# The chunk's whole decay: four small matmuls, or the last row of the running sum turned by a transfer

## Chip, cores and metric

The kernel runs on one core of one Trainium2 chip. The metric is the device time of one execution in microseconds (us). A core has TensorE (PE, with its weight loads shown as PEld), VectorE (DVE), ScalarE (ACT), GpSimd (POOL) and SyncE (SP, which here only issues transfers); each works off its own instructions in order.

## The reference, cut to what matters

```python
# q, k, v, f_logit: (4, 8, 768, 48)  float32;  w_in: (384, 2048);  w_out: (2048, 384)
f = 1.0 / (1.0 + np.exp(-f_logit))
for t in range(S):
    state = f[:, :, t, :, None] * state + np.einsum('bhd,bhe->bhde', k[:, :, t], v[:, :, t])
    y[:, :, t] = np.einsum('bhd,bhde->bhe', q[:, :, t], state)
x = y.transpose(0, 2, 1, 3).reshape(B * S, H * D)     # (3072, 384)
h = x @ w_in
out = np.maximum(0.01 * h, h) @ w_out
```

A gated linear attention (a state of 48 x 48 for each head, that decays by a gate for each of its rows) is followed by a two-layer network with a leaky ReLU.

## The kernel before

The 768 steps are cut into 6 chunks of 128. A unit `u` is one chunk `c` of one batch `b`; there are 24, ordered by chunk and then by batch, so unit 0 to 3 is the first chunk of the four batches. A unit's tile has the 128 steps on the partitions and 8 heads x 48 columns.

For each unit:

- `load` (L82 to L89) issues four transfers of 192 KB from SP: `f_raw`, `k_raw`, `q_raw`, `v_raw`.
- `gate_act`: ScalarE forms `lf = ln(1 + exp(-f))`, which is minus the logarithm of the gate. `lf` has 64 columns for each head, the last 16 zero.
- `gate_pe` (L113): one matmul with an upper triangle of ones gives the running sum of `lf` over the steps in PSUM, `cs[:, 0:384]` (L117). Four more matmuls (L120), one for each pair of heads, take `lf` of the pair as weights and a column of ones as the moving operand. Each writes one column of `cs`: the sum over the whole chunk, with the 2 x 64 features of the pair on the partitions. The last chunk needs no such sum, so 20 units of 24 do this.
- `decay_act` (L124): ScalarE reads `cs` and writes `em_t = exp(cs)`, `a_t = exp(-cs)`, and `a_end = exp(-)` of the four added columns (L133).
- `scale_pool`: GpSimd multiplies `kh = k * em_t` (L139), `qh = q * a_t` (L140) and casts `v` (L142).
- `turn_pe`, `turn_dve`, `score_pe`, `mask_dve`, `mix_pe`, `state_pe`: transposes of `kh` and `qh` (L149), scores (L168), the causal mask, and the output `y` and the chunk's addition to the state.
- `state_dve` adds it to the state `sf`; `state_pool` (L216) multiplies `sf` by `a_end`, broadcast along the free dimension (L221), and casts it (L222).
- `up` and `down`: the two layers (L250, L259), with ScalarE's leaky ReLU from PSUM (L252); `put` copies the result and stores it from SP (L265).

The order on every engine is written out by hand, with no reordering. In the prologue SP issues `load(0)` to `load(4)`; then come `gate`, `decay` and `scale` of units 0 and 1, and the rest of unit 0 with `state_pool(0)`. The loop `for i in range(24)` works on several units at once: it issues `load(i+5)`, turns unit i+1, does the first half of `up(i)`, scores i+1, does `gate_pe`, `decay_act` and `scale_pool` of unit i+2, the second half of `up(i)`, `mix_pe`, `y_act`, `state_pe`, `state_dve` and `state_pool` of i+1, `gate_act` of i+3, `down(i)` with the transposes `x_pe(i+1)` (L233) in its middle, and `put(i)`. So GpSimd has, in this order: `scale_pool(0)`, `scale_pool(1)`, `state_pool(0)`, `scale_pool(2)`, `state_pool(1)`, `scale_pool(3)`, and so on.

The PSUM tiles `cs`, `py`, `pt` and `px` of a pass share a ring of two buffers (`tag="sm"`): `pt` (L203) takes the buffer that `cs` leaves.

Of the kernel before, what the change touches and what calls it, by code (L numbers as in the profile page):

```python
# [9 lines left out]
FP32 = mybir.dt.float32  # L10
BF16 = mybir.dt.bfloat16
AF = mybir.ActivationFunctionType
# [3 lines left out]
def kernel(  # L16
# [10 lines left out]
    nc = tc.nc  # L27

    B, H, S, D = q.shape
    assert (B, H, S, D) == (4, 8, 768, 48)  # L30
    C = 128
    NCH = S // C
    P2 = H // 2
# [7 lines left out]
    const = ctx.enter_context(tc.tile_pool(name="const", bufs=1))  # L41
    inp = ctx.enter_context(tc.tile_pool(name="inp", bufs=6))
    work = ctx.enter_context(tc.tile_pool(name="work", bufs=3))
# [14 lines left out]
    make_upper_triangular(nc, ut, val=1.0, diag=True)  # L58
    ident = const.tile([128, 128], BF16, tag="ident")
    make_identity(nc, ident)  # L60
    ones_col = const.tile([128, 1], BF16, tag="ones")
    nc.gpsimd.memset(ones_col, 1.0)

    w_in_b = const.tile([128, NK, FF], BF16, tag="w_in")
    w_out_b = const.tile([128, NF, KD], BF16, tag="w_out")
# [2 lines left out]
    lfs = [const.tile([128, H, 64], BF16, name=f"lf{i}", tag=f"lf{i}") for i in range(3)]  # L68
    qhs = [const.tile([128, H, 64], BF16, name=f"qh{i}", tag=f"qh{i}") for i in range(3)]
    khs = [const.tile([128, H, 64], BF16, name=f"kh{i}", tag=f"kh{i}") for i in range(3)]  # L70
    qbds = [const.tile([128, P2, 2, 128], BF16, name=f"qbd{i}", tag=f"qbd{i}") for i in range(2)]
    state_f = [const.tile([128, P2, D], FP32, name=f"sf{b}", tag=f"sf{b}") for b in range(B)]
    state_b = [const.tile([128, P2, D], BF16, name=f"sb{b}", tag=f"sb{b}") for b in range(B)]
    for t in lfs + qhs + khs + qbds:
        nc.vector.memset(t, 0.0)
    for t in state_f:
        nc.vector.memset(t, 0.0)


# [23 lines left out]
    st = {}  # L103
# [9 lines left out]
    def gate_pe(u):  # L113
        c, b = units[u]
        lf = lfs[u % 3]
        cs = ps_s.tile([128, 512], FP32, name="cs", tag="sm")
        nc.tensor.matmul(cs[:, 0:H * D], ut, lf[:, :, 0:D], start=True, stop=True)  # L117
        if c < NCH - 1:
            for p in range(P2):
                nc.tensor.matmul(cs[:, H * D + p:H * D + p + 1], lf[:, 2 * p:2 * p + 2, :], ones_col,  # L120
                                 start=True, stop=True)
        st[u] = {"cs": cs}

    def decay_act(u):  # L124
        c, b = units[u]
        cs = st[u]["cs"]
        a_t = work.tile([128, H, D], BF16, name="a_t", tag="a_t")
        em_t = work.tile([128, H, D], BF16, name="em_t", tag="em_t")
        nc.scalar.activation(em_t, cs[:, 0:H * D], AF.Exp, scale=1.0)  # L129
        nc.scalar.activation(a_t, cs[:, 0:H * D], AF.Exp, scale=-1.0)  # L130
        if c < NCH - 1:
            a_end = work.tile([128, P2], FP32, name="a_end", tag="a_end")
            nc.scalar.activation(a_end, cs[:, H * D:H * D + P2], AF.Exp, scale=-1.0)  # L133
            st[u]["a_end"] = a_end
        st[u]["a"], st[u]["em"] = a_t, em_t

    def scale_pool(u):
# [78 lines left out]
    def state_pool(u):  # L216
        c, b = units[u]
        if c == NCH - 1:
            return
        sf = state_f[b]  # L220
        nc.gpsimd.tensor_mul(sf, sf, st[u]["a_end"][:, :, None].to_broadcast([128, P2, D]))  # L221
        nc.gpsimd.tensor_copy(out=state_b[b], in_=sf)  # L222

    def y_act(u):
# [54 lines left out]
    gate_act(0)  # L279
    gate_act(1)  # L280
    gate_pe(0)
    decay_act(0)
    scale_pool(0)
    gate_pe(1)
    decay_act(1)
    scale_pool(1)
    gate_act(2)
# [6 lines left out]
    y_act(0)  # L294
    state_dve(0)
    state_pool(0)
    x_pe(0)
    x_dve(0)

    for i in range(NU):  # L300
# [11 lines left out]
        if n2 < NU:  # L312
            gate_pe(n2)
            decay_act(n2)
            scale_pool(n2)
        up(i, 2)
        up(i, 3)
        if n1 < NU:
            mix_pe(n1)
            y_act(n1)  # L320
            state_pe(n1)
            state_dve(n1)
            state_pool(n1)
# [38 lines left out]
```

## Time and profile before

| what | value |
|---|---|
| median of 3 runs | 212.48 us (212.34 to 213.68) |
| the profiled execution | 211.29 us, of which 209.4 us are the span from the first to the last instruction |
| PE busy | 177.8 us (85%) |
| PE weight loads busy | 146.1 us (70%) |
| ACT busy | 108.7 us (52%) |
| DVE busy | 97.4 us (46%) |
| POOL busy | 76.8 us (37%) |
| HBM read, written | 25.17 MB, 4.72 MB |

The profile was taken on one execution; the 1.89 us outside the span lie before the first and after the last instruction. Busy shares are means over the whole span, and the beginning differs from the rest: in the first 33 us the transfers of weights and inputs run at 176 GB/s and PE is busy for 4.77 us; from 41.5 us to 167.8 us PE is busy without a break. A matmul's end is modelled, so PE's busy time is not PE at its peak.

### The profile page before, as it was taken

To read this page: it belongs to the slowest core of one execution; us is meant where nothing else is said; L and a number is where in the kernel's file an instruction comes from. 1 tells how busy PE (TensorE), PEld (TensorE's weight loads), DVE (VectorE), ACT (ScalarE), POOL (GpSimd) and SP (SyncE) were. 2 spreads that over 40 slices of the span, in tenths; PEclk is the share of its full clock that TensorE was granted. 3 is DMA by queue.
4 is the path that set the end of the run, shared out by engine and by line. 5 is a ranking of instruction groups with operands and counts; after the bars stand their busy time and mean duration, and the time that the engine had idled before them with its cause. 6 is when DMAs were issued, how large, how long until landed. Compare 5 with 4: busy or idle time off the path is not lost.

```text
span 209.4 us, 5831 instructions
## 1 busy us (share of the span) xinstructions
PE 177.8 (85%) x2432; PEld 146.1 (70%) x2432; DVE 97.4 (46%) x223; ACT 108.7 (52%) x237; POOL 76.8 (37%) x129
## 2 busy tenths in 40 slices
PE   0000149999999999999999999999999999999993
PEld 0000028788779788877988887798888778877881
DVE  8000044466546545654654565465455545633511
ACT  4000332775576458447645845774585567555540
POOL 8300071542553255145325524532552454034000
PEclk9999999999999999999999999999999999999999
DMA  6999999998796479568647846956695681100111
GB/s 114 171 195 184 199 191 189 156 219 163 121 176 143 105 136 177 114 118 163 147 102 133 186 111 116 157 116 141 128 187 113 119 153 41 38 28 18 38 41 38
DMA packets 106267, 27.12 MB, mean 130 GB/s; under 512 B 100352, under 2 KB 105472, under 8 KB 106240
## 3 DMA queue, kind: packets, MB, share of 16 engines
q1 hardware_dynamic: 103296, 23.60, 59.5%
q0 software_dynamic: 2944, 3.15, 9.0%
q8 instruction: 19, 0.31, 0.6%
q14 instruction: 8, 0.07, 0.1%
HBM read 25.17 MB, written 4.72 MB: 143 GB/s over the span
## 4 chain that ended last, share of the span: by engine, by line
PE 83%; issue 10%; POOL 4%; DVE 1%; ACT 0%; POOLq 0%
PE pm L250 32%; PE pm L259 30%; PE pw L168 6%; PE tp L149 5%; PE py L191 2%; PE px L233 2%; PE py L187 2%; PE cs L117 2%; PE pt L203 2%; POOL w_in_b L94 2%; POOL w_out_b L99 1%; POOL kh L139 1%; PE cs L120 1%; DVE wm L175 1%; POOL qh L140 1%
## 5 line engine op out<-in xcount | busy, mean ns | idle before, releaser
L252 ACT ACTIVATE gT<-pm 128x512 bf16<-128x512 f32 x96 | 56.2, 601 | 64.1 <-PE pm L250 62.3
L250 PE MATMUL pm<-xT,w_in_b 128*128 128x128 bf16 x1152 | 73.4, 221 | 0.0
L259 PE MATMUL pm<-w_out_b,gT 128*128 128x384 bf16 x384 | 70.1, 326 | 0.0
L250 PEld LDWEIGHTS <-w_in_b 128*128 128x128 bf16 x1152 | 67.2, 99 | 0.6
L139 POOL TENSOR_TENSOR kh<-k_raw,em_t 128x384 bf16<-128x384 f32 x24 | 22.0, 916 | 110.5 <-ACT em_t L129 105.7
L259 PEld LDWEIGHTS <-gT 128*128 128x128 bf16 x384 | 35.2, 98 | 18.8
L175 DVE TENSOR_TENSOR wm<-pw,ut 128x512 bf16<-128x512 f32 x48 | 30.9, 686 | 12.7 <-PE pw L168 11.9
L117 PE MATMUL cs<-lf,ut 128*128 128x384 bf16 x24 | 8.1, 339 | 24.9 <-ACT lf L111 24.9
L264 DVE COPY osb<-pm 128x384 f32<-128x384 f32 x24 | 13.4, 558 | 26.6 <-PE pm L259 26.6
L109 ACT ACTIVATE e_t<-f_raw 128x384 f32<-128x384 f32 x24 | 12.9, 536 | 23.7 <-DMA f_raw<-in_f_logit_dram 23.7
L120 PEld LDWEIGHTS <-lf 128*128 128x128 bf16 x80 | 5.0, 99 | 25.2 <-issue 23.8
L140 POOL TENSOR_TENSOR qh<-q_raw,a_t 128x384 bf16<-128x384 f32 x24 | 21.9, 914 | 0.0
L155 DVE COPY kT<-tp 128x512 bf16<-128x512 bf16 x24 | 10.0, 415 | 23.6 <-PE tp L149 23.6
L238 DVE COPY xT<-px 128x384 bf16<-128x384 bf16 x24 | 8.6, 358 | 22.2 <-PE px L233 22.2
L213 DVE TENSOR_TENSOR sf<-sf,pt 64x192 f32<-64x192 f32 x20 | 6.9, 346 | 22.2 <-PE pt L203 22.2
L168 PE MATMUL pw<-qbd,kT 128*128 128x256 bf16 x96 | 14.8, 277 | 1.3 <-DVE qbd L158 1.3
L129 ACT ACTIVATE em_t<-cs 128x384 bf16<-128x384 f32 x24 | 11.8, 491 | 4.5 <-PE cs L120 3.7
L111 ACT ACTIVATE lf<-e_t 128x384 bf16<-128x384 f32 x24 | 12.5, 523 | 0.8
L168 PEld LDWEIGHTS <-kT 128*128 128x128 bf16 x96 | 9.4, 99 | 4.3 <-DVE kT L155 0.8
L226 ACT CAST xn<-py 128x384 bf16<-128x384 f32 x24 | 11.4, 474 | 1.5 <-PE py L191 1.5
L142 POOL CAST v_b<-v_raw 128x384 bf16<-128x384 f32 x24 | 12.1, 505 | 0.0
L130 ACT ACTIVATE a_t<-cs 128x384 bf16<-128x384 f32 x24 | 11.6, 485 | 0.0
(37 smaller groups left out, 155.3 us busy)
## 6 DMA issues: line engine op xcount, KB each, us to landing
f_raw<-in_f_logit_dram SPq DMA_DIRECT2D x24, 192.0 KB, 3.2
k_raw<-in_k_dram SPq DMA_DIRECT2D x24, 192.0 KB, 3.8
q_raw<-in_q_dram SPq DMA_DIRECT2D x24, 192.0 KB, 4.0
v_raw<-in_v_dram SPq DMA_DIRECT2D x24, 192.0 KB, 4.3
out_dram<-osb SPq DMA_DIRECT2D x24, 192.0 KB, 2.0
w_in_b<-in_moe_w_in_dram POOLq DMA_DIRECT2D x6, 256.0 KB, 8.8
w_out_b<-in_moe_w_out_dram POOLq DMA_DIRECT2D x2, 768.0 KB, 18.2
```

The costliest lines, as they stand in the source:

```text
L109: nc.scalar.activation(e, f, AF.Exp, scale=-1.0)
L111: nc.scalar.activation(lf[:, :, 0:D], e, AF.Ln, bias=1.0)
L117: nc.tensor.matmul(cs[:, 0:H * D], ut, lf[:, :, 0:D], start=True, stop=True)
L139: nc.gpsimd.tensor_mul(khs[u % 3][:, :, 0:D], r["k"], st[u]["em"])
L140: nc.gpsimd.tensor_mul(qhs[u % 3][:, :, 0:D], r["q"], st[u]["a"])
L142: nc.gpsimd.tensor_copy(out=v_b, in_=r["v"])
L168: nc.tensor.matmul(pw[:, 2 * i:2 * i + 2, :], kT[:, p, :], qbd[:, p, :, :], start=True, stop=True)
L175: nc.vector.tensor_mul(wm, pw, ut[:, None, :].to_broadcast([128, 4, 128]))
L250: nc.tensor.matmul(pm[:, i, :], w_in_b[:, kk, ff * 128:(ff + 1) * 128], s["xT"][:, kk, :], start=(kk == 0), stop=(kk == NK - 1))
L252: nc.scalar.activation(s["g"][:, 4 * g:4 * g + 4, :], pm, AF.Prelu, alpha=0.01)
L259: nc.tensor.matmul(s["pm2"], s["g"][:, ff, :], w_out_b[:, ff, :], start=(ff == 0), stop=(ff == NF - 1))
L264: nc.vector.tensor_copy(out=osb, in_=st[u]["pm2"])
```

## The change

The four matmuls on a column of ones go. The last row of the running sum already holds the sum over the chunk, but with the features along the free dimension of partition 127. ScalarE takes the exponential of the last 32 rows of `cs` (partitions 96 to 127) into a float32 tile `a_row`, written so that in each row the 128 features of a pair stand apart by four elements and the four pairs side by side. A transfer on SP's queue then moves row 127 (128 x 4 numbers, 2 KB) to a tile `a_ends` with one feature on each partition and four numbers in each. `state_pool` reads that tile. There are three `a_row` and four `a_ends` buffers, cleared by VectorE at the start.

```diff
-    ones_col = const.tile([128, 1], BF16, tag="ones")
-    nc.gpsimd.memset(ones_col, 1.0)
...
+    a_ends = [const.tile([128, P2], FP32, name=f"ae{i}", tag=f"ae{i}") for i in range(4)]
+    a_rows = [const.tile([128, 128, P2], FP32, name=f"ar{i}", tag=f"ar{i}") for i in range(3)]
-    for t in lfs + qhs + khs + qbds:
+    for t in a_ends + lfs + qhs + khs + qbds:
         nc.vector.memset(t, 0.0)
-    for t in state_f:
+    for t in state_f + [t[96:128] for t in a_rows]:
         nc.vector.memset(t, 0.0)
...
         nc.tensor.matmul(cs[:, 0:H * D], ut, lf[:, :, 0:D], start=True, stop=True)
-        if c < NCH - 1:
-            for p in range(P2):
-                nc.tensor.matmul(cs[:, H * D + p:H * D + p + 1], lf[:, 2 * p:2 * p + 2, :], ones_col,
-                                 start=True, stop=True)
...
         if c < NCH - 1:
-            a_end = work.tile([128, P2], FP32, name="a_end", tag="a_end")
-            nc.scalar.activation(a_end, cs[:, H * D:H * D + P2], AF.Exp, scale=-1.0)
-            st[u]["a_end"] = a_end
+            a_row = a_rows[u % 3]
+            nc.scalar.activation(a_row[96:128].rearrange("t (i e) p -> t p i e", i=2)[:, :, :, 0:D],
+                                 cs[96:128, 0:H * D].rearrange("t (p i d) -> t p i d", p=P2, i=2),
+                                 AF.Exp, scale=-1.0)
+            nc.sync.dma_start(out=a_ends[u % 4], in_=a_row[127:128])
...
-        nc.gpsimd.tensor_mul(sf, sf, st[u]["a_end"][:, :, None].to_broadcast([128, P2, D]))
+        nc.gpsimd.tensor_mul(sf, sf, a_ends[u % 4][:, :, None].to_broadcast([128, P2, D]))
```

## The prediction, made before the changed kernel ran

> **What bounds the kernel now.** I read the page first, for the engine that ends last.
>
> ```profile
> PE 177.8 (85%) x2432; PEld 146.1 (70%) x2432; DVE 97.4 (46%) x223; ACT 108.7 (52%) x237; POOL 76.8 (37%) x129
> PE 83%; issue 10%; POOL 4%; DVE 1%; ACT 0%; POOLq 0%
> ```
>
> The second line is the chain that ended last: 83% of it is PE. After the start-up PE never idles until the last units, so PE time removed there shortens the run, and another engine matters only where PE comes to wait for it. Next I read the timeline over two passes of the loop. Passes i = 0 to 17 compute the whole decay of unit i+2; from i = 18 the unit is of the last chunk and the L120 matmuls are absent, while all else of pass 18 is there. So the profile of before already has a pass with the matmuls gone:
>
> ```profile
> 158.40 1.50 PE L250 MATMUL pm<-xT,w_in_b 128*128 128x128 bf16 x24
> ...
> 159.88 0.60 PE L168 MATMUL pw<-qbd,kT 128*128 128x256 bf16 x4
> 160.31 0.33 PE L117 MATMUL cs<-lf,ut 128*128 128x384 bf16 x1
> 160.47 0.24 PE L120 MATMUL cs<-ones_col,lf 128*128 128x1 bf16 x4
> 160.58 1.50 PE L250 MATMUL pm<-xT,w_in_b 128*128 128x128 bf16 x24
> ...
> 165.70 1.50 PE L250 MATMUL pm<-xT,w_in_b 128*128 128x128 bf16 x24
> ...
> 167.18 0.60 PE L168 MATMUL pw<-qbd,kT 128*128 128x256 bf16 x4
> 167.61 0.33 PE L117 MATMUL cs<-lf,ut 128*128 128x384 bf16 x1
> 167.78 1.50 PE L250 MATMUL pm<-xT,w_in_b 128*128 128x128 bf16 x24
> ...
> 168.73 1.18 ACT L252 ACTIVATE gT<-pm 128x512 bf16<-128x512 f32 x2
> ...
> 169.81 0.47 ACT L226 CAST xn<-py 128x384 bf16<-128x384 f32 x1
> ...
> 170.83 0.32 PEld L233 LDWEIGHTS <-xn 128*128 128x128 bf16 x3
> ```
>
> Each line is start, duration, engine, source line. From the scores (L168) to the next `up` (L250) pass 17 takes 160.58 - 159.88 = 0.70 us, pass 18 takes 167.78 - 167.18 = 0.60. The whole pass falls from 165.70 - 158.40 = 7.30 to 7.20 (the next pass opens at 172.90). Four L120 matmuls cost PE 0.10 us, not the 4 x 0.16 of their own durations: they are pipelined.
>
> Last I read the start, because the change puts a transfer into SP's queue and makes GpSimd wait for it.
>
> ```profile
> 33.17 0.51 POOL L221 TENSOR_TENSOR sf<-sf,a_end 128x192 f32<-128x192 f32 x1 [2.86 <-DVE sf L214]
> ...
> 36.44 0.98 SPq L87 DMA_DIRECT2D v_raw<-in_v_dram  x1
> 37.47 1.00 SPq L87 DMA_DIRECT2D f_raw<-in_f_logit_dram  x1
> ...
> 37.80 0.92 POOL L139 TENSOR_TENSOR kh<-k_raw,em_t 128x384 bf16<-128x384 f32 x1 [3.71 <-ACT em_t L129]
> 38.67 0.92 POOL L140 TENSOR_TENSOR qh<-q_raw,a_t 128x384 bf16<-128x384 f32 x1
> ```
>
> ```profile
> v_raw<-in_v_dram SPq DMA_DIRECT2D x1, 192.0 KB, 5.5
> f_raw<-in_f_logit_dram SPq DMA_DIRECT2D x1, 192.0 KB, 5.5
> ```
>
> The first fence shows SP still issuing the prologue's loads at 36.44 us: that `v_raw` is the last transfer of load(4), and the `f_raw` at 37.47 opens load(5). The second, the transfers issued in that stretch, gives 5.5 us from issue to landing for both. The first state multiply (L221, unit 0) ran at 33.17, before SP reached the place where the change puts unit 0's transfer.
>
> **The change part by part.**
>
> *Removed: 80 L120 matmuls and their weight loads.* 18 passes x 0.10 us. The gain of pass 0 falls ahead of the stall worked out below and is swallowed by it; 17 x 0.10 = 1.7 us remain. The eight in the prologue (units 0, 1) lie under waits for transfers and are worth nothing. From both sides: the weight-load row puts pass 18's gap at as little as 0.08, so 1.4 to 1.8.
>
> *Replaced on ScalarE: 20 exponentials of 128x4 by 20 of 32x384.* The old one's row is 0.18 us, but the next instruction starts 0.05 after it (161.51 to 161.57), so it costs the queue almost nothing. The new one has the free size of `a_t`, which starts 0.39 after `em_t` and is followed 0.37 later. No row shows an exponential that writes float32 16 bytes apart. Lower bound 0.37; upper bound 0.60, the mean duration of the 128x512 L252 with nothing overlapped. I take 0.37, since the element count is `a_t`'s. What it makes late: the two L252 and `xn` (L226). Set on pass 18: `xn` ends at 169.81 + 0.47 + 0.37 = 170.65, and PE loads it at 170.83; a hand-over takes 0.05 (ACT's `xn` of 32.05 ends at 32.53, PE starts at 32.58), so 0.13 us of cover is left and the edit costs nothing. At 0.60 the cover is gone and PE waits 0.10 per pass, 1.7 us in all. `cs` is also held longer: the new read ends about 169.2, and `pt`, which takes that buffer, starts at 169.52. Hidden.
>
> *Added on VectorE and taken from GpSimd at the start:* seven clears (three of 32x512 float32, four of 128x4) for one of 0.10 us. VectorE ends its clears near 5.2 us and first works at 28.37 (23 us of idle); by the rows of L75 and L77 (0.22 to 0.49 each) seven cost under 3.5 us, hidden there. The four that come first delay `lf`'s clear (0.86 to 1.68), which ScalarE needs at 4.28. Nothing.
>
> *Added on SP: 20 transfers of 2 KB.* Each waits for ScalarE. What is queued behind it is load(i+5) or the store `put(i)`. In the loop it stands after load(i+5) and before `put(i)`, for which SP waits anyway (89.3 us over 21 times in SP's list of waits), so the wait replaces a part of a longer one. GpSimd needs unit i+2's numbers a pass later: the exponential ends near 161.9 in pass 17, SP has issued `v_raw` by 162.3, 4.3 us (the median landing of `v_raw`) gives 166.6, and `state_pool` would read at 163.56 + 7.2 = 170.8. Four us of cover. Their 2,560 packets stand against 103,296: no bandwidth.
>
> *At the start that cover isn't there.* The program places the transfers of units 0 and 1 after load(4), so SP issues unit 0's at 37.47, though ScalarE has had the row since about 26.6. When it lands is the term that decides. The nearest rows: `v_raw` just ahead lands at 36.44 + 5.5 = 41.9, `f_raw` issued at this very place at 37.47 + 5.5 = 43.0; the store in SP's queue at 42.59 landed after 3.5 us, 46.1, 0.6 after the `v_raw` ahead of it (41.78 + 3.7 = 45.5), though later such stores, with nothing ahead, took 2.0 (median). So a transfer lands in the order of the queue. I take 42.3; bounds 39.5 (37.47 + 2.0, a free queue) and 43.0.
>
> The Trainium skill, in "DMA: Bandwidth & Descriptors", section "Queues, rings and completion order", says that each DMA engine consumes a queue's descriptors in ring order, yet that completion isn't first in, first out for the issuing engine; the same page's section on the anatomy of one DMA puts the fixed cost at about 2.0 us. By the fixed cost alone the sum would end at 211.3 us, by the landing rows at 214.1; the rows show a full queue and I follow them.
>
> GpSimd works in order, so `scale_pool(2)` stands behind `state_pool(0)`. With a landing at L: L221 starts at L + 0.05, L222 0.57 later (39.99 to 40.56 in a later pass), `kh` of unit 2 0.30 after that, `qh` 0.87 after (37.80 to 38.67), and `qh` takes 0.91. It is ready at L + 2.70 = 45.0, where before it was ready at 39.6. PE's transposes of unit 2 stood at 41.53 and 41.75, and `up(1)` at 41.98, 0.23 after the `qh` transposes. Now `up(1)` starts at L + 2.70 + 0.05 + 0.23 = L + 2.98 = 45.3. That is 3.3 us late (L - 39.0), and PE is the bound from there on. Unit 1's numbers follow unit 0's by a fraction of a us and are needed only after `scale_pool(2)`; unit 2's, behind load(5), land near 47 and are needed past 50. One stall, then.
>
> *The sum.* 211.29 + 3.3 - 1.7 = 212.9 us for an execution like the profiled one (span 209.4 to 211.0). The median of the runs stands 1.19 higher, so 212.48 + 1.6 = 214.1 us, 0.8% more than before.
>
> **A price that the trace shows only at the start: cold matmuls.** PE would idle from 41.5 to 44.2 and again until 45.1.
>
> ```profile
> 33.73 2.77 PE L250 MATMUL pm<-xT,w_in_b 128*128 128x128 bf16 x24
> ...
> 37.05 1.50 PE L250 MATMUL pm<-xT,w_in_b 128*128 128x128 bf16 x24
> ```
>
> The same 24 matmuls take 2.77 us just after the waits of the prologue and 1.50 once PE has run on; the granted clock reads 1.00 in both stretches. A stall could bring one such slow stretch back: 0 to 1.27 us. The idle time before the slow stretch was spread over 30 us, the new one is under 4 us, so I take 0 and keep 1.27 for the range. The skill's page "TensorE: Matmul & The Clock Gate", section "Why this matters for your kernels", asks for no idle gap above about 3 us, as a window of idle halves the clock; the gap of 2.7 us here is under that, and by the rule a landing half a us later would add the 1.27.
>
> **The rivals.**
>
> 1. *The stall comes and PE turns slow.* 214.1 + 1.27 = 215.4 us. For: the 2.77 us row. Against: a gap shorter than any that the trace shows ahead of slow matmuls.
> 2. *The other side: the transfer doesn't queue.* If its 2 KB land 2.0 us after issue, L = 39.5, `up(1)` is 0.5 late, and the gain of 1.7 wins: 212.48 + 0.5 - 1.7 = 211.3 us. It decides wherever L lies below 40.7, where L - 39.0 equals 1.7. For: the stores' median of 2.0, and few bytes. Against: the store at 42.59, which took 3.5 behind loads.
> 3. *The 128 runs of 16 bytes are slow.* All on one DMA engine, at the mean packet of the main queue (59.5% of 16 x 209.4 us over 103,296 packets, 19 ns), they take 2.5 us more: L = 44.8, 216.6 us. For: the source is one partition. Against: nothing in the trace shows an uneven split.
> 4. *ScalarE becomes the wait in every pass.* At 0.60 for the new exponential: 214.1 + 1.7 = 215.8 us. For: 0.13 us of cover is thin. Against: three rows of this size are followed after 0.37 to 0.39.
>
> **How the numbers follow.** Forecast 0.46, rival 1 0.20, rival 2 0.13, rival 3 0.11, rival 4 0.10. The likeliest time is 214.1; its own range, from the gain's 1.4 to 1.8 and a landing of 41.9 to 43.0, is 213.6 to 215.1. The range of all reaches down past half of the way to rival 2 and up past rival 3 with a little of the slow clock: 212.0 to 217.0. A measurement here tells about 1% from no change: below 210.4 is faster, above 214.6 slower. Faster 0.05 (rival 2 with nothing left of the 0.5). Slower 0.48: a third of the forecast's own range, nearly all of rivals 1, 3 and 4. Within 1% 0.47.
>
> **What would show each step right or wrong.** Passes of 7.20 us in place of 7.30 from the second to the 18th; L221's first start moving from 33.17 to 42 or later, its releaser a DMA; `kh` of unit 2 at 43 instead of 37.80; one wait on PE before the qh transposes, near 45; `xn` still ready before PE loads it; an ACT group of 32x384 near 0.49 us. If L221 starts before 40.7 the forecast is wrong and rival 2 holds; if the 24 matmuls after the stall take more than 2 us, rival 1; if PE shows a wait for `xn` in each pass, rival 4.

## The result: 2.6% slower, and the profile after

The changed kernel takes 218.01 us (median of 4 runs, 217.57 to 218.78) against 212.41 for the kernel before in the same comparison: a ratio of 1.0264, with a 95% interval of 1.0201 to 1.0328. That is above the range of 212.0 to 217.0. The profiled execution took 217.57 us, with a span of 215.8. Some executions of one kernel run over a per cent longer than its others in a slower state; the ratios here and below leave those out, and need not be the quotients of the medians given beside them, which include them.

Two lines of the page after the change: the busy time of each engine, and each engine's share of the chain of work that ended last:

```profile
PE 179.7 (83%) x2352; PEld 143.6 (67%) x2352; DVE 99.1 (46%) x230; ACT 125.9 (58%) x237; POOL 76.6 (36%) x128
PE 66%; ACT 14%; issue 10%; POOL 6%; DMA 2%; DVE 1%; ACTq 0%; POOLq 0%
```

ScalarE's share of the chain went from 0% to 14%; its busy time rose by 17.2 us with as many instructions as before. The groups of instructions by shape (last columns: busy us, mean ns of one, idle time before them and what ended it) show where the time went:

```profile
L131 ACT ACTIVATE ar<-cs 32x384 f32<-32x384 f32 x20 | 17.3, 863 | 0.5
L126 ACT ACTIVATE a_t<-cs 128x384 bf16<-128x384 f32 x24 | 11.6, 484 | 0.0
L221 POOL TENSOR_TENSOR sf<-sf,ae 128x192 f32<-128x192 f32 x20 | 10.1, 507 | 15.3 <-DMA ae<-ar 11.3 <-DVE sf L214 4.1
L203 PE MATMUL pt<-v_b,kh 128*128 128x96 bf16 x80 | 6.8, 208 | 3.6 <-ACT ar L131 3.6
```

The added exponential (L131) takes 863 ns, where `a_t` with as many numbers in a row takes 484. PE now waits for it in `pt` (L203), and GpSimd waits once, 11.3 us, for a transfer (L221). Pass 17 in the timeline:

```profile
165.77 0.60 PE L168 MATMUL pw<-qbd,kT 128*128 128x256 bf16 x4
166.20 0.33 PE L117 MATMUL cs<-lf,ut 128*128 128x384 bf16 x1
166.37 1.50 PE L250 MATMUL pm<-xT,w_in_b 128*128 128x128 bf16 x24
167.01 0.48 ACT L126 ACTIVATE a_t<-cs 128x384 bf16<-128x384 f32 x1
167.52 0.87 ACT L131 ACTIVATE ar<-cs 32x384 f32<-32x384 f32 x1
168.41 1.08 ACT L252 ACTIVATE gT<-pm 128x512 bf16<-128x512 f32 x2
168.44 0.33 PE L203 MATMUL pt<-v_b,kh 128*128 128x96 bf16 x4 [0.17 <-ACT ar L131]
...
169.38 0.48 ACT L226 CAST xn<-py 128x384 bf16<-128x384 f32 x1
...
169.92 0.17 PEld L233 LDWEIGHTS <-xn 128*128 128x128 bf16 x3 [0.24 <-ACT xn L226]
171.85 1.50 PE L250 MATMUL pm<-xT,w_in_b 128*128 128x128 bf16 x24
```

The same places in pass 18 of before, which has no third exponential:

```profile
168.36 0.48 ACT L130 ACTIVATE a_t<-cs 128x384 bf16<-128x384 f32 x1
...
168.73 1.18 ACT L252 ACTIVATE gT<-pm 128x512 bf16<-128x512 f32 x2
...
169.52 0.33 PE L203 MATMUL pt<-v_b,kh 128*128 128x96 bf16 x4
```

The gain is there: L168 to L250 is 166.37 - 165.77 = 0.60 us. But from `a_t` to the L252 pair it is now 168.41 - 167.01 = 1.40 us, where pass 18 of before had 168.73 - 168.36 = 0.37. `pt` starts 168.44 - 166.20 = 2.24 us after L117 (1.91 before), as it must wait until L131 has read `cs`. The passes open 7.55 us apart instead of 7.30.

The start, in the same timeline:

```profile
36.58 1.48 SPq L134 DMA_DIRECT2D ae<-ar  x2
...
40.47 0.51 POOL L221 TENSOR_TENSOR sf<-sf,ae 128x192 f32<-128x192 f32 x1 [11.28 <-DMA ae<-ar]
...
41.34 0.91 POOL L139 TENSOR_TENSOR kh<-k_raw,em_t 128x384 bf16<-128x384 f32 x1
...
42.21 0.91 POOL L140 TENSOR_TENSOR qh<-q_raw,a_t 128x384 bf16<-128x384 f32 x1
...
42.31 0.40 PE L149 MATMUL tp<-ident,kh 128*128 128x128 bf16 x4 [1.11 <-POOL kh L139]
...
43.18 0.40 PE L149 MATMUL tp<-ident,qh 128*128 128x128 bf16 x4 [0.47 <-POOL qh L140]
...
43.41 1.50 PE L250 MATMUL pm<-xT,w_in_b 128*128 128x128 bf16 x24
```

This is the forecast chain: SP issues the first transfer behind load(4), GpSimd's state multiply waits for it, `kh` and `qh` of unit 2 stand behind, and PE waits.

**The spans, split.** I cut each profile at the first start of `up(0)` and at that of `up(1)`:

| us | before | after | difference |
|---|---|---|---|
| `up(0)` starts | 33.73 | 32.62 | -1.11 |
| `up(0)` to `up(1)` | 8.25 | 10.79 | +2.54 |
| `up(1)` to `up(18)`, 17 passes | 123.72 | 128.44 | +4.72 |
| the rest | 43.70 | 43.95 | +0.25 |
| span | 209.4 | 215.8 | +6.4 |

The 2.54 us are not all stall: 1.95 of them stand at the transposes that wait for `kh` and `qh` (2.07 in a second profile of the changed kernel, a0_after), and 0.45 are `pt` waiting for the new exponential in pass 0 as well. And a profile is one execution. In the medians, 218.01 - 212.41 = 5.60 us; the stretch from `up(1)` to the end explains 4.72 + 0.25 = 4.97 of them (in the two profiles of the changed kernel it lasts 172.4 and 172.3 us), so that for the start only about 0.6 us are left.

So there are rival accounts, which the expectations below call theories; each says what its A and B stand for in its run. In the main, theory A has two parts: passes that are longer because the writes 16 bytes apart make the exponential dear, and a stall at the start from the place in SP's queue. Theory B puts the exponential's length down to its type or its partitions, and holds that the start hangs on the loads whatever the order. Theory C is that only the wait for the buffer of `cs` costs PE time.

### The profile page after: what moved, and what is told of

It is laid out like the page before. It is cut to its first block, busy times and chain, and to the rows that moved or that the text cites. A ratio compares the mean times of both kernels' runs of the same rounds, so it can differ in the third digit from the quotient of the medians.

```text
span 215.8 us, 5716 instructions
## 1 busy us (share of the span) xinstructions
PE 179.7 (83%) x2352; PEld 143.6 (67%) x2352; DVE 99.1 (46%) x230; ACT 125.9 (58%) x237; POOL 76.6 (36%) x128
## 3 DMA queue, kind: packets, MB, share of 16 engines
HBM read 25.17 MB, written 4.72 MB: 138 GB/s over the span
## 4 chain that ended last, share of the span: by engine, by line
PE 66%; ACT 14%; issue 10%; POOL 6%; DMA 2%; DVE 1%; ACTq 0%; POOLq 0%
PE pm L259 28%; PE pm L250 19%; ACT ar L131 7%; PE pw L168 6%; PE tp L149 5%; ACT em_t L125 4%; ACT a_t L126 3%; PE pt L203 3%; PE px L233 2%; PE cs L117 2%; DMA ae<-ar 2%; POOL w_in_b L94 2%; POOL qh L140 1%; POOL kh L139 1%; POOL w_out_b L99 1%
## 5 line engine op out<-in xcount | busy, mean ns | idle before, releaser
L252 ACT ACTIVATE gT<-pm 128x512 bf16<-128x512 f32 x96 | 55.1, 596 | 55.6 <-PE pm L250 53.4
L250 PE MATMUL pm<-xT,w_in_b 128*128 128x128 bf16 x1152 | 73.4, 221 | 0.0
L259 PE MATMUL pm<-w_out_b,gT 128*128 128x384 bf16 x384 | 70.1, 326 | 0.0
L250 PEld LDWEIGHTS <-w_in_b 128*128 128x128 bf16 x1152 | 68.6, 99 | 2.0
L259 PEld LDWEIGHTS <-gT 128*128 128x128 bf16 x384 | 35.2, 98 | 18.8
L117 PE MATMUL cs<-lf,ut 128*128 128x384 bf16 x24 | 8.1, 339 | 23.9 <-ACT lf L111 23.9
L109 ACT ACTIVATE e_t<-f_raw 128x384 f32<-128x384 f32 x24 | 13.0, 542 | 21.5 <-DMA f_raw<-in_f_logit_dram 21.5
L149 PEld LDWEIGHTS <-kh 128*128 128x128 bf16 x96 | 7.5, 101 | 25.2 <-POOL kh L139 22.5
L131 ACT ACTIVATE ar<-cs 32x384 f32<-32x384 f32 x20 | 17.3, 863 | 0.5
L168 PE MATMUL pw<-qbd,kT 128*128 128x256 bf16 x96 | 15.0, 280 | 1.3 <-DVE qbd L158 1.3
L221 POOL TENSOR_TENSOR sf<-sf,ae 128x192 f32<-128x192 f32 x20 | 10.1, 507 | 15.3 <-DMA ae<-ar 11.3
L168 PEld LDWEIGHTS <-kT 128*128 128x128 bf16 x96 | 9.5, 100 | 4.4 <-DVE kT L155 0.8
```

The costliest lines, as they stand in the source:

```text
L109: nc.scalar.activation(e, f, AF.Exp, scale=-1.0)
L131: nc.scalar.activation(a_row[96:128].rearrange("t (i e) p -> t p i e", i=2)[:, :, :, 0:D], cs[96:128, 0:H * D].rearrange("t (p i d) -> t p ...
L149: nc.tensor.transpose(tp[:, i, p, :], src[:, 2 * p:2 * p + 2, :], ident)
L168: nc.tensor.matmul(pw[:, 2 * i:2 * i + 2, :], kT[:, p, :], qbd[:, p, :, :], start=True, stop=True)
L250: nc.tensor.matmul(pm[:, i, :], w_in_b[:, kk, ff * 128:(ff + 1) * 128], s["xT"][:, kk, :], start=(kk == 0), stop=(kk == NK - 1))
L252: nc.scalar.activation(s["g"][:, 4 * g:4 * g + 4, :], pm, AF.Prelu, alpha=0.01)
```

## The experiments

Ratios are against the kernel before, run beside them. Its median moved between 211.66 and 212.91 from one set of runs to the next, so times are compared within a set.

**Removal alone (e4_gone).**

```diff
-            for p in range(P2):
-                nc.tensor.matmul(cs[:, H * D + p:H * D + p + 1], lf[:, 2 * p:2 * p + 2, :], ones_col,
-                                 start=True, stop=True)
...
-            nc.scalar.activation(a_end, cs[:, H * D:H * D + P2], AF.Exp, scale=-1.0)
+            nc.scalar.activation(a_end, cs[:, 0:P2], AF.Exp, scale=-1.0)
```

> The kernel before without the 80 small matmuls; a_end is the exponential of four columns of the running sum instead, of the same size and in the same place. It leaves out the sum over the whole chunk. It gives the gain that the change could have at most from TensorE. Theory A: passes 7.20 us instead of 7.30, time 212.4 - 18 x 0.10 = 210.6 us. Theory B (the matmuls lay under other waits and only the modelled ends make a difference between passes 17 and 18): 212.4 us.

Measured: passes of 7.20 us; from `up(1)` to the end 165.71 us instead of 167.42, 1.71 less. Time 211.26 against 212.79, ratio 0.9961 (0.9911 to 1.0011), which by itself does not exclude no change; the passes do. The term of 17 x 0.10 was right.

**The writes put side by side (e2_flat).**

```diff
-            nc.scalar.activation(a_row[96:128].rearrange("t (i e) p -> t p i e", i=2)[:, :, :, 0:D],
-                                 cs[96:128, 0:H * D].rearrange("t (p i d) -> t p i d", p=P2, i=2),
+            nc.scalar.activation(a_row[96:128].rearrange("t (h y) p -> t h (y p)", h=H)[:, :, 0:D],
+                                 cs[96:128, 0:H * D],
                                  AF.Exp, scale=-1.0)
```

> The changed kernel, with the added exponential writing its 384 numbers of a row in runs of 48, next to each other, instead of 16 bytes apart; the transfer is unchanged, so the state's decay takes its numbers in another arrangement (that arrangement is what the kernel changes of the computation). Theory A (the spacing of the writes makes the exponential 0.87 us long, and that makes PE wait in each pass): exponential 0.49 us, passes 7.20 us, the start's stall of 2.5 us stays, time 218.0 - 17 x 0.35 = 212.0 us. Theory B (its length comes from the float32 output or from the 32 partitions): exponential 0.87, time 218.0.

Its group by shape:

```profile
L131 ACT ACTIVATE ar<-cs 32x384 f32<-32x384 f32 x20 | 9.7, 483 | 0.5
```

483 ns, passes 7.20 us, 212.36 against 212.79: ratio 1.0000 (0.9961 to 1.0039). `pt` no longer waits. The extra length of L131 is the spacing of its writes, and it carries the loss of the passes. One thing more: the two passes of the first chunk that follow the stall, which have no state matmuls, take 7.16 and 7.17 us here and 7.00 in e4_gone. Even the short exponential is felt there.

**Other spacings (e3_bf16 and e10_read).** In e3_bf16 the two tiles become bfloat16, so the writes stand 8 bytes apart. In e10_read the destination stays and the order of the walk is turned:

```diff
-            nc.scalar.activation(a_row[96:128].rearrange("t (i e) p -> t p i e", i=2)[:, :, :, 0:D],
-                                 cs[96:128, 0:H * D].rearrange("t (p i d) -> t p i d", p=P2, i=2),
+            nc.scalar.activation(a_row[96:128].rearrange("t (i e) p -> t i e p", i=2)[:, :, 0:D, :],
+                                 cs[96:128, 0:H * D].rearrange("t (p i d) -> t i d p", p=P2, i=2),
```

> The changed kernel, with a_row and a_ends in bfloat16: the same order of writes, four elements apart, but 8 bytes apart instead of 16, and runs of 8 bytes in the transfer. Theory A, if the distance in bytes counts: an exponential between 0.49 and 0.87 us and a pass between 7.20 and 7.55; if any write that isn't next to the last costs the same: 0.87 us and 218.0 us. Theory B (float32 output is what costs): 0.49 us and 212.0 us.

> The changed kernel with the added exponential going through its 384 numbers in the order of the destination: writes next to each other (runs of 192), reads from PSUM 384 bytes apart; same numbers in the same places, all else the same. Theory A (only the spacing of the writes is dear): exponential 0.49 us, passes 7.20 as in e2_flat, 212.4 us at a median of 212.7 for the kernel before. Theory B (any spaced side of the instruction costs): exponential 0.8 us or more, passes 7.5 or more, 218 us.

The groups, first e3_bf16, then e10_read:

```profile
L131 ACT ACTIVATE ar<-cs 32x384 bf16<-32x384 f32 x20 | 20.5, 1024 | 0.5
```

```profile
L131 ACT ACTIVATE ar<-cs 32x384 f32<-32x384 f32 x20 | 9.7, 483 | 0.5
```

Neither expectation for e3_bf16 held: half the distance made it longer, 1024 ns, with passes of 7.71 us and 221.18 us (ratio 1.0423, 1.0359 to 1.0486). e10_read writes the same numbers to the same places, reads them 384 bytes apart, and costs 483 ns: 212.84 us, ratio 1.0025 (0.9980 to 1.0071). Float32 output and the 32 partitions are excluded as causes; in these runs spaced writes are dear, and spaced reads from PSUM are not. Why 8 bytes cost more than 16 is not shown: the type changed with the distance.

**A longer ScalarE order without holding `cs` (e5_sbuf).**

```diff
 # on top of e2_flat; zt is a cleared SBUF tile
             nc.sync.dma_start(out=a_ends[u % 4], in_=a_row[127:128])
+            dump = work.tile([128, H * D], BF16, name="dump", tag="dump")
+            nc.scalar.activation(dump, zt, AF.Exp, scale=-1.0)
```

> The kernel e2_flat with one more exponential of 128x384 on ScalarE right after the added one, from a zeroed SBUF tile into a tile that nobody reads: ScalarE's order gets about 0.38 us longer, as by the writes 16 bytes apart, but the PSUM buffer of the running sum is not held longer. Theory A (two places have the same price: pt waits for the buffer, and without that wait xn would be late by as much): no wait of pt, xn late, passes near 7.55 instead of 7.20, time 212.4 + 17 x 0.34 = 218.1 us. Theory C (the buffer alone is the cause): passes 7.20, 212.4 us.

From the list of waits (total us, times, longest):

```profile
PEld L236 <- ACT xn L229: 13.8, 19, 0.8
PE px L236 <- ACT xn L229: 6.7, 19, 0.4
```

No wait of `pt`, and PE waits for `xn` 19 times. The dummy costs ScalarE's order 0.55 us rather than 0.38; passes are 7.72 us, the time 221.00 (ratio 1.0455, 1.0386 to 1.0524). A pass grows by 0.52 for 0.55 more on ScalarE, as in the changed kernel by 0.35 for 0.38. So the buffer ring is not needed for the loss: without it `xn` is late instead. In the changed kernel both places want nearly the same delay of PE, and it is paid once: in pass 17 `pt` is 0.33 us late, `xn` ends at 169.38 + 0.48 = 169.86, and the transposes that read it start at 169.92, 1.31 us after the first L259, where pass 18 of before had 1.30.

**The start: another order (e1_order, e1_again) and another queue (e6_poolq).** e1_order, and e1_again beside the changed kernel (a0_after):

```diff
-    state_pool(0)
     x_pe(0)
...
             scale_pool(n2)
+            if i == 0:
+                state_pool(0)
```

> The changed kernel, with state_pool(0) moved behind scale_pool(2) in GpSimd's order; nothing else. Theory A (the loss is one stall at the start, where kh and qh of unit 2 stand behind a wait for the first transfer, and a longer pass after it): the stall of 2.5 us goes, up(0) to up(1) takes about 8.3 us instead of 10.8, passes stay at 7.55, time 218.0 - 2.5 = 215.5 us. Theory B (the start is bound by the loads, PE waits for them anyway): time stays at 218.0 within 0.5.

> The kernel e1_order again, with more rounds, since four runs did not tell a difference of under a microsecond from none. Theory A: 0.6 to 1.7 us less than the changed kernel beside it. Theory B: no difference.

> The changed kernel again, with more rounds, beside e1_again on the same chip. Theory A: 5.0 us of longer passes and end, and 0.6 to 1.7 us of stall over the kernel before: 217.3 to 218.4 at a median of 211.7.

e6_poolq is e2_flat with `nc.gpsimd.dma_start` behind the cast of `v` in `scale_pool`:

> The kernel e2_flat with the transfer issued on GpSimd's queue behind scale_pool instead of SP's queue behind the loads. Theory A (the queue of SP delays the first transfers): unit 0's numbers land about 2 to 3 us after about 30 us, the first state multiply waits for no transfer, up(0) to up(1) takes 8.0 us, time lower than e2_flat's 212.4 by the part of the stall that a usual start leaves, 0.6 us: 211.8. Theory B (the DMA engines themselves are full until then, whatever the queue): the first state multiply still waits until about 41 us and the time is 212.4.

Its first state multiply, in the timeline:

```profile
33.41 0.50 POOL L222 TENSOR_TENSOR sf<-sf,ae 128x192 f32<-128x192 f32 x1 [1.71 <-DVE sf L215]
```

On GpSimd's own queue the numbers are there when VectorE has added the state; the transfer is not waited for. So the delay was the place in SP's queue, not full DMA engines. The time is 210.78 us, ratio 0.9962 (0.9917 to 1.0006), against e2_flat's 1.0000; these intervals overlap, so the gain in time is not proved.

The order alone removed the wait as well (in both profiles `kh` of unit 2 goes first), but not the time: 217.82 us (ratio 1.0270, 1.0200 to 1.0341) and 218.64 (1.0254, 1.0205 to 1.0302), where the changed kernel has 218.01 (1.0264) and, beside e1_again, 218.34 (a0_after: 1.0249, 1.0208 to 1.0291). In its two profiles `up(0)` started at 35.78 and 35.68, in those of the changed kernel at 32.62 and 34.70.

**The stall alone (e9_stall).**

```diff
 # on top of the kernel before; state_pool reads a_ends
-            st[u]["a_end"] = a_end
+            nc.sync.dma_start(out=a_ends[u % 4], in_=a_end)
```

> The kernel before, with its four matmuls and its small exponential, and one transfer more: a_end goes through SP's queue from SBUF to SBUF into the tile that state_pool reads. It isolates the wait at the start. Theory A (the stall has a price of its own): passes 7.28 to 7.30 us as before, the first state multiply waits for the transfer until about 41 us, 0.6 to 1.7 us more than before (212.3 to 213.4 at a median of 211.7). Theory B (what e1_order suggests: no price): the same time as before.

215.74 against 212.72: ratio 1.0116 (1.0068 to 1.0164), more than expected. The state multiply started at 42.26, PE waited 3.01 us for `kh`, and then:

```profile
44.10 0.40 PE L150 MATMUL tp<-ident,kh 128*128 128x128 bf16 x4 [3.01 <-POOL kh L140]
...
45.20 2.69 PE L251 MATMUL pm<-xT,w_in_b 128*128 128x128 bf16 x24
```

The stretch from 45 to 49 us (its length, the busy time of PE, PEld, DVE, ACT and POOL with their instructions, then the granted clock, the DMA share and GB/s):

```profile
45.00:49.00 4.00, 4.00 (x40) 3.67 (x41) 1.81 (x5) 1.19 (x2) 1.17 (x3) 0.57 1.07 201
```

This execution paid 11.38 - 8.25 = 3.1 us more between `up(0)` and `up(1)` and, at a granted clock of 0.57, another 1.5 us in pass 1: rival 1's mechanism, which the changed kernel did not show (its wait for `kh` was 1.11 us and its 24 matmuls took 1.50). In v1_row, below, the wait was 1.91 us, and the 24 matmuls took 1.50 too. The Trainium skill's rule in "TensorE: Matmul & The Clock Gate", section "Why this matters for your kernels", of no gap above about 3 us, agrees with these three cases.

**No exponential at all (v1_row, v2_row_order).**

```diff
 # decay_act: no third exponential. scale_pool, behind the cast of v:
+        if units[u][0] < NCH - 1:
+            a_row = a_rows[u % 3]
+            nc.gpsimd.tensor_copy(out=a_row[96:128].rearrange("t (i e) p -> t p i e", i=2)[:, :, :, 0:D],
+                                  in_=st[u]["a"][96:128].rearrange("t (p i) d -> t p i d", i=2))
+            nc.sync.dma_start(out=a_ends[u % 4], in_=a_row[127:128])
```

v2_row_order adds the order of e1_order.

> No exponential of its own for the last row: GpSimd copies the last 32 rows of a_t (which ScalarE writes anyway, in bfloat16) into a_row behind the cast of v, four elements apart and in float32, and the transfer follows as in the changed kernel. Theory A (ScalarE's longer order is the whole loss of the passes; GpSimd has 3.8 us of idle time in a pass): passes 7.20 us, no wait for xn, the start's stall stays; 212.4 + 0.6 - 1.7 = 211.3 us. Theory B (a transfer per pass costs something by itself): passes longer than 7.20, 212 us or more.

> v1_row with state_pool(0) behind scale_pool(2) in GpSimd's order. Theory A: the stall at the start goes as well, up(0) to up(1) near 8.0 us; 0.6 us less than v1_row, 210.7 us, and less than both kernels. Theory B (PE's first work comes later by as much when the stall goes, since both hang on the loads): the same as v1_row.

v1_row: 211.79 us, ratio 1.0032 (0.9998 to 1.0067). v2_row_order: 210.12, ratio 0.9921 (0.9878 to 0.9964), faster than the kernel before by 0.8% and than the changed kernel. From `up(1)` to the end they take 165.93 and 165.99 us: a transfer in each pass costs nothing in the passes (7.20 us, as without it). The group of GpSimd's copy in v2_row_order:

```profile
L141 POOL CAST ar<-a_t 32x384 f32<-32x384 bf16 x20 | 17.5, 874 | 1.2
```

It is as slow as the exponential was, but on an engine that has the time.

## Why the prediction was wrong

**The step that failed is "replaced on ScalarE", an edit costed at nothing.** I took 0.37 us for what the new exponential adds between `a_t` and L252, with an upper bound of 0.60. It adds 1.40 - 0.37 = 1.03. Of that, 0.38 is the spacing of the writes (863 against 483 ns). The other 0.65 is there in e2_flat too, as its pass 17 shows:

```profile
162.08 0.48 ACT L126 ACTIVATE a_t<-cs 128x384 bf16<-128x384 f32 x1
...
162.59 0.48 ACT L131 ACTIVATE ar<-cs 32x384 f32<-32x384 f32 x1
...
163.10 1.08 ACT L252 ACTIVATE gT<-pm 128x512 bf16<-128x512 f32 x2
```

`a_t` to L131 takes 0.51 and L131 to L252 another 0.51, since this instruction did not overlap with its neighbours, while `em_t` to `a_t` takes 0.39. The upper bound was a row of more elements, but of side-by-side writes; no row of the trace showed spaced ones, so it was no bound.

The cover was mis-sized too, the other way. By my sum (0.37 + 0.13 of cover) an exponential that adds 0.65 would cost 0.15 us a pass; in e2_flat it costs nothing in the passes of 7.20. I had measured the cover at PE's load of `xn`. There that load starts 1.26 us after the first L259 (1.14 before), and the transposes behind it at 1.31 (1.30 before).

**"`cs` is held longer, hidden" failed with it.** I had the read ending about 1.6 us after L117; it ended 2.2 us after, and `pt` was due at 1.91.

**Rival 4 named the mechanism, in the main:** ScalarE becomes the wait in every pass, though where PE itself idles is `pt` (for the buffer) and not `xn`. Its price of 1.7 us was the mis-sized term: the passes lost 4.72 where they should have gained 1.7, a swing of 6.4 us.

**The gain was right:** 0.10 us a pass (e4_gone). **The clears on VectorE and the transfers in the loop were hidden as said:** after the first one, no state multiply waited for a transfer.

**The stall was right in its chain; its size is not a constant.** `up(1)` starts 2.94 us after the first state multiply in the changed kernel and 2.94 or 2.95 in a0_after, v1_row and e9_stall; I had L + 2.98, with that multiply at L + 0.05. In the profiled execution the landing was at 40.3, not 42.3: the transfer was issued earlier (36.58, not 37.47) and took 3.76 us, not 4.8. In a0_after it took 4.21 and landed at 41.6, and over the eleven profiles with this transfer on SP's queue it took 2.8 to 4.7. So 42.3 was within what happens, but high. The fixed cost of about 2.0 us that the prediction quotes from the Trainium skill, "DMA: Bandwidth & Descriptors", stands there in a section on transfers issued from GpSimd ("Anatomy of one DMA"); on SP's queue the shortest took 1.9 in the changed kernel, and the first one was not among the short ones.

**The sum added a whole stall to the median, where about 0.6 us were left for it.** e10_read, which has passes of 7.20 us and an exponential of 0.48 as forecast, has a ratio of 1.0025 (up to 1.0071); the forecast's was 214.1 / 212.48 = 1.0076. So the forecast would have come out too high even with the passes as it had them.

**The offset to the median was not a constant.** I added 1.19 us to the profiled execution's time. Over fourteen profiles of these kernels `up(0)` starts anywhere from 32.62 to 35.79 us, always 9.4 us after unit 1's first exponential (L109 in the kernel before), which waits for that unit's `f_raw`: issued near 4 us, it lands between 23.2 and 26.4. The profile of before, at 33.73, was an early one. A wait for a given landing costs a late start less. So the stall's worth differs: 1.7 us between v1_row and v2_row_order, 2.5 to 3.0 in e9_stall with its slow matmuls, nothing visible between the changed kernel and e1_order. In all three profiles with the order of e1_order, `up(0)` is at 35.7 to 35.8. That `f_raw` had landed by 26.4, before any engine reached the place that this order changes, so the engines' order does not delay `up(0)`; why the load landed late all three times is not shown.

Also open: why L131 overlaps with neither neighbour even with side-by-side writes. The 0.25 us by which the rest of the span is longer goes with the transfers on SP's queue, not with the exponential: from the start of the last store to the end it is 2.73 or 2.74 us in before, e4_gone and e6_poolq, which have none there, and 2.98 to 3.06 in the other eleven profiles. What is done in that time is not shown.

## What to carry to other kernels

An instruction moved onto an engine in order has to be priced with its write pattern, not only its size: where two loops can be walked in either order, let the writes be adjacent and the reads spaced, and measure it (e10_read: two access patterns, and the ratio falls from 1.0264 to 1.0025). Before an added instruction is called hidden, measure the cover at every consumer behind it, the release of its source buffer included. In these runs a small transfer behind large loads landed 0.2 to 1.8 us after the last of them; what an in-order engine has queued behind the wait sets the most that it can cost, and a late start of the consumer makes it less.

## What the runs showed of the hardware

On ScalarE, 32x384 from PSUM took 483 ns with adjacent writes, in either layout; 863 with float32 written 16 bytes apart; 1024 with bfloat16 written 8 bytes apart. Reading PSUM 384 bytes apart cost nothing (483 ns in e10_read). GpSimd's copy from bfloat16 to float32 with 16-byte spacing took 874 ns for 32x384, where its cast of 128x384 from float32 to bfloat16 into adjacent places takes about 500; the types differ, so the spacing is not shown to be the cause there. A 2 KB transfer in SP's queue took 1.9 us at the least and 3.8 at most in the changed kernel.
